# x + alpha * fx on one Trainium2 core: the first store held for 13 units of an addition, and a new order and placing of the loads

## The chip, the cores and the metric

The kernel runs on one core of a Trainium2 chip. The metric is the time of one execution in device microseconds (us). The core has 16 DMA engines that move data between its DRAM and its on-chip memory SBUF (128 partitions), and compute engines of which this kernel uses VectorE (DVE in the profile) for nearly all of its arithmetic. SyncE (SP) issues every transfer here. SP goes through its instructions in order: one that waits holds up all behind it.

## The reference

```python
B, S, D = 512, 32, 640            # x and fx: bf16; alpha: one bf16 number
def reference(x, fx, alpha):
    return x + alpha * fx
```

Each of x, fx and the output has 512 x 32 x 640 bf16 elements, 20.97 MB. Nothing is used twice, so 41.94 MB have to be read and 20.97 MB written.

## The kernel before

All three tensors are seen as 128 rows, one for each partition, and each row is cut into N = 160 units of K = 512 elements (1 KiB). One SBUF tile, `buf`, has room for ALL = 207 units in each partition, fewer than the 320 of both inputs, so places are used again. The tables F and X (lines 17 and 18) say where units of fx and of x stand: (first unit, end, home in buf). `at` (line 79) turns a range of units into a slice of `buf` by them. The last two pieces of each table are put over places whose fx units an earlier addition has read: those loads wait for that addition.

The order of the work is written out by hand, as lines of `PLAN` (line 23). Each line is one step, and the steps are emitted top to bottom:

- `f` and `x` issue a load of fx or x from SP (lines 88 and 92); in the kernel before, the number is the piece's place in the table. `s` issues a store (line 108) of a range in the table S.
- `a` loads alpha and brings it to all 128 partitions with one small matrix product (lines 110 to 118).
- `m a b` multiplies units a to b of fx by alpha in place, on VectorE (line 97).
- `t a b` adds fx's units a to b to x's in place, on VectorE (line 104). What the stores write are these sums, out of x's homes.

Each engine takes its steps in the order of PLAN. Waits follow from the data: a multiplication waits for its load, an addition for its load and the multiplication, a load for the last reader of the place that it overwrites, a store for the additions of its range. All transfers share one queue, so the DMA engines take them in the order of issue, each engine eight rows (partitions) of every transfer. A row is one contiguous piece of DRAM: a load of 64 units has 128 rows of 64 KiB, one of 32 units has rows of 32 KiB.

Up to the last load the DMA engines see this order: fx 0 to 8, fx 8 to 64, alpha, x 0 to 64, fx 64 to 96, x 64 to 96, fx 96 to 128, x 96 to 128, fx 128 to 160, x 128 to 160; then the stores of units 0 to 64, 64 to 128 and 128 to 160. The first store's data are complete early, when the additions `t 32 64` and `t 0 32` are through. On SP it stands right behind the last load.

Of the kernel before, what the change touches and what calls it, by code (L numbers as in the profile page):

```python
# [1 line left out]

# [4 lines left out]

ACT = mybir.ActivationFunctionType
ALU = mybir.AluOpType
F32 = mybir.dt.float32  # L10
BF16 = mybir.dt.bfloat16

K = 512
P = 128


F = [(0, 8, 96), (8, 64, 104), (64, 96, 160), (96, 128, 128), (128, 160, 175)]
X = [(0, 64, 0), (64, 96, 64), (96, 128, 96), (128, 160, 143)]
S = [(0, 64), (64, 128), (128, 160)]
N = 160  # L20
ALL = 207

PLAN = """
f 0
f 1
a
x 0
f 2
x 1
m 0 64  # L30
t 32 64
t 0 32
f 3
x 2
m 64 96
t 79 96
f 4
t 64 79
m 96 128
t 111 128  # L40
x 3
t 96 111
m 128 160
t 128 160
s 0
s 1
s 2
"""


@with_exitstack
def kernel(
    ctx: ExitStack,
    tc: tile.TileContext,
    x: bass.AP,
    fx: bass.AP,
    alpha: bass.AP,
    out: bass.AP,
):
    nc = tc.nc  # L60
    xv = x.flatten_outer_dims().rearrange("(p n) d -> p (n d)", p=P)
    fxv = fx.flatten_outer_dims().rearrange("(p n) d -> p (n d)", p=P)
    ov = out.flatten_outer_dims().rearrange("(p n) d -> p (n d)", p=P)
    assert xv.shape[1] == N * K

    consts = ctx.enter_context(tc.tile_pool(name="consts", bufs=1))
    psum = ctx.enter_context(tc.tile_pool(name="psum", bufs=1, space=bass.MemoryType.PSUM))
    whole = ctx.enter_context(tc.tile_pool(name="whole", bufs=1))
    ctx.enter_context(tc.manual_schedule())

    sync = mybir.DependencyInfo(mybir.DependencyClass.Sync, mybir.DependencyReason.DATA)
    buf = whole.tile([P, ALL * K], x.dtype, name="buf")
    done = []
    lanes = {}

    def units(v, a, b):
        return v[:, a * K : b * K]

    def at(pieces, a, b):

        s, _, h = next(p for p in pieces if p[0] <= a < p[1])
        e, _, g = next(p for p in pieces if p[0] < b <= p[1])
        assert h - s == g - e
        return units(buf, a + h - s, b + h - s)

    def load_f(i):
        a, b, _ = F[i]
        done.append(nc.sync.dma_start(out=at(F, a, b), in_=units(fxv, a, b)))  # L88

    def load_x(i):  # L90
        a, b, _ = X[i]
        done.append(nc.sync.dma_start(out=at(X, a, b), in_=units(xv, a, b)))

    def multiply(a, b):
        term = at(F, a, b)
        done.append(
            nc.vector.tensor_scalar(  # L97
                out=term, in0=term, scalar1=lanes["a_f"][:], scalar2=None, op0=ALU.mult
            )
        )  # L100

    def total(a, b):
        s = at(X, a, b)
        done.append(nc.vector.tensor_tensor(out=s, in0=s, in1=at(F, a, b), op=ALU.add))  # L104

    def store(i):
        a, b = S[i]
        done.append(nc.sync.dma_start(out=units(ov, a, b), in_=at(X, a, b)))

    def alpha_to_lanes():  # L110
        a_1 = consts.tile([1, 1], alpha.dtype, name="a_1")
        done.append(nc.sync.dma_start(out=a_1[:], in_=alpha[None, :]))  # L112
        ones = consts.tile([1, P], alpha.dtype, name="ones")
        nc.vector.memset(ones[:], 1.0)  # L114
        a_ps = psum.tile([P, 1], F32, name="a_ps")
        done.append(nc.tensor.matmul(a_ps[:], ones[:], a_1[:], start=True, stop=True))  # L116
        lanes["a_f"] = consts.tile([P, 1], F32, name="a_f")
        nc.vector.tensor_copy(out=lanes["a_f"][:], in_=a_ps[:])  # L118

    does = {  # L120
        "f": load_f,
        "x": load_x,
        "a": alpha_to_lanes,
        "m": multiply,
        "t": total,
        "s": store,
    }
    for step in PLAN.split("\n"):
        if step:
            what, *of = step.split()  # L130
            does[what](*map(int, of))

    rest = nc.sync.nop(nofuse=True)
    for i in done[:-1]:
        tc.add_manual_dep(rest.ins, i.ins.name, sync, reason="all but the last store")


# [1 line left out]
_INS = ['x', 'fx', 'alpha']  # L139
_OUTS = [((512, 32, 640), 'bfloat16')]  # L140


# [23 lines left out]
```

## Time and profile before

The median of three runs is 151.65 us (151.59 to 151.67). The profile below is of one execution.

| what | value |
|---|---|
| time of the profiled execution | 151.67 us |
| its span | 149.89 us |
| DMA engines busy | 98.0% of the span |
| bytes moved | 62.92 MB, 420 GB/s over the span |
| VectorE busy | 65.9 us (44%), 13 instructions |
| additions: 32, 17, 15 units | 8.69, 4.69, 4.15 us each |
| multiplications: 64, 32 units | 8.75, 4.48 us each |

How to read what follows: the page gives busy time of each engine, then the span in 40 slices with a digit for each (tenths of the slice), then the DMA queue, then the chain of waits that ended last. In the list in order of time, a line has the start, the duration, the engine, the line of the kernel, the operation and what it writes and reads; "SPq" lines are issues of transfers, whose rows move later. A table of windows gives, for each stretch between two times, the busy time of each engine and how many instructions began there, the granted clock, the mean busy share of the DMA engines and the rate in GB/s. Bytes are counted where a row starts, so windows that hold whole rows are the ones to compare.

### The profile page before, as it was taken

The page shows a single profiled execution, that of the slowest core. Times are in us where ns is not written, and L with a number is a line of the kernel's source. Part 1 is how long each engine was busy: PE and PEld are TensorE (multiplying, and loading weights), DVE is VectorE, ACT ScalarE, POOL GpSimd, SP SyncE. Part 2 cuts the span into 40 slices and gives each one's busy share as a digit, 9 for nine tenths or more (in the row PEclk, how much of TensorE's full clock was granted, in tenths as well). Part 3 has the DMA queues.
Part 4 walks back from the last instruction along what each step waited for, and adds up shares of the span by engine and source line. Part 5 has one row for each costly group of instructions (what it writes and reads, how often), then busy time and mean ns, then how long its engine had stood idle before and what let it go on. Part 6 is the DMA issues. An engine that isn't in the chain of part 4 may idle for free.

```text
span 149.9 us, 84 instructions
## 1 busy us (share of the span) xinstructions
PE 0.2 (0%) x1; PEld 0.1 (0%) x1; DVE 65.9 (44%) x13; POOL 0.2 (0%) x4
## 2 busy tenths in 40 slices
PE   0000000000000000000000000000000000000000
PEld 0000000000000000000000000000000000000000
DVE  0000009930079999999954998309920000000000
POOL 0000000000000000000000000000000000000000
DMA  5979996969899999999999999998998969697994
GB/s 164 606 337 398 490 525 280 560 280 560 376 437 437 428 420 420 420 420 420 428 463 463 437 437 428 420 420 367 472 490 350 560 280 560 280 560 315 455 446 184
DMA packets 1730, 62.92 MB, mean 420 GB/s; under 512 B 194, under 2 KB 194, under 8 KB 194
## 3 DMA queue, kind: packets, MB, share of 16 engines
q1 hardware_dynamic: 1730, 62.92, 98.0%
HBM read 41.94 MB, written 20.97 MB: 420 GB/s over the span
## 4 chain that ended last, share of the span: by engine, by line
DMA 51%; DVE 20%; SPq 1%; issue 0%; DVEq 0%
DMA buf<-in_x_dram 51%; DVE buf L104 20%; SPq L88 1%; SPq L112 0%; DVEq L104 0%
## 5 line engine op out<-in xcount | busy, mean ns | idle before, releaser
L104 DVE TENSOR_TENSOR buf<-buf 128x16384 bf16<-128x16384 bf16 (+2 forms) x7 | 43.5, 6251 | 20.5 <-DMA buf<-in_x_dram 20.5
L97 DVE TENSOR_SCALAR buf<-buf,a_f 128x16384 bf16<-128x16384 bf16 (+1 forms) x4 | 22.2, 5550 | 0.9 <-DMA buf<-in_fx_dram 0.9
L118 DVE COPY a_f<-a_ps 128x1 f32<-128x1 f32 x1 | 0.2, 157 | 21.5 <-PE a_ps L116 21.5
L114 DVE MEMSET ones<- 1x128 bf16 x1 | 0.2, 165 | 0.8 <-PEq L150 0.8
L116 PE MATMUL a_ps<-a,ones 1*128 1x1 bf16 x1 | 0.2, 158 | 22.3 <-DMA a<-in_alpha_dram 22.3
L150 POOL MEMSET const-bfloat16-1.0<- 128x1 bf16 x1 | 0.1, 101 | 0.0
L150 POOL MEMSET const-uint8-127<- 128x1 uint8 x1 | 0.1, 101 | 0.0
L150 POOL MEMSET const-float32-0.0<- 128x1 f32 x1 | 0.1, 98 | 0.2 <-issue 0.2
L150 POOL MEMSET const-float32-1.0<- 128x1 f32 x1 | 0.1, 98 | 0.0
L116 PEld LDWEIGHTS <-ones 1*128 1x128 bf16 x1 | 0.1, 97 | 1.0 <-DVE ones L114 1.0
## 6 DMA issues: line engine op xcount, KB each, us to landing
buf<-in_fx_dram SPq DMA_DIRECT2D x3, 4096.0 KB, 22.0
buf<-in_x_dram SPq DMA_DIRECT2D x3, 4096.0 KB, 21.4
buf<-in_fx_dram SPq DMA_DIRECT2D x1, 7168.0 KB, 21.4
out_dram<-buf SPq DMA_DIRECT2D x1, 4096.0 KB, 39.5
buf<-in_fx_dram SPq DMA_DIRECT2D x1, 1024.0 KB, 4.9
out_dram<-buf SPq DMA_DIRECT2D x2, 49.8
a<-in_alpha_dram SPq DMA_DIRECT2D x1, 0.0 KB
buf<-in_x_dram SPq DMA_DIRECT2D x1, 39.9
```

The source lines that it names most:

```text
L88: done.append(nc.sync.dma_start(out=at(F, a, b), in_=units(fxv, a, b)))
L97: nc.vector.tensor_scalar(out=term, in0=term, scalar1=lanes["a_f"][:], scalar2=None, op0=ALU.mult)
L104: done.append(nc.vector.tensor_tensor(out=s, in0=s, in1=at(F, a, b), op=ALU.add))
L114: nc.vector.memset(ones[:], 1.0)
L116: done.append(nc.tensor.matmul(a_ps[:], ones[:], a_1[:], start=True, stop=True))
L118: nc.vector.tensor_copy(out=lanes["a_f"][:], in_=a_ps[:])
L150: nc = _bacc.Bacc("TRN2", target_bir_lowering=False, num_devices=1)
```

## The change

There are four parts. Units 64 to 128 of fx come in one load instead of two. The places in `buf` are other ones: fx 0 to 64 at 128, fx 64 to 128 at 64, fx 128 to 160 at 111; x 64 to 128 at 143 and x 128 to 160 at 79. The order of the steps follows from that: the loads are now fx 0 to 8, fx 8 to 64, alpha, x 0 to 64, fx 64 to 128, x 96 to 128, x 64 to 96, fx 128 to 160, x 128 to 160, and an addition of 15 units (64 to 79), cut into 13 and 2, is left over until after the multiplication of the last units. And the first store gets a wait that its data do not ask for: `LATE` ties the issue of `s 0 64` to the end of `t 64 77`. Steps now name unit ranges instead of places in tables. The rest is another spelling: each step returns its instruction, which is kept under the step's text so that `LATE` can find it.

```diff
-F = [(0, 8, 96), (8, 64, 104), (64, 96, 160), (96, 128, 128), (128, 160, 175)]
-X = [(0, 64, 0), (64, 96, 64), (96, 128, 96), (128, 160, 143)]
-S = [(0, 64), (64, 128), (128, 160)]
+F = [(0, 64, 128), (64, 128, 64), (128, 160, 111)]
+X = [(0, 64, 0), (64, 128, 143), (128, 160, 79)]
 N = 160
 ALL = 207
 
 PLAN = """
-f 0
-f 1
+f 0 8
+f 8 64
 a
-x 0
-f 2
-x 1
+x 0 64
+f 64 128
 m 0 64
 t 32 64
+x 96 128
 t 0 32
-f 3
-x 2
-m 64 96
+x 64 96
+m 64 128
+t 111 128
+f 128 160
+t 96 111
 t 79 96
-f 4
-t 64 79
-m 96 128
-t 111 128
-x 3
-t 96 111
+x 128 160
 m 128 160
+t 64 77
+t 77 79
+s 0 64
 t 128 160
-s 0
-s 1
-s 2
+s 64 128
+s 128 160
 """
+LATE = {"s 0 64": "t 64 77"}
...
+    def transfer(name, out, in_):
+        r = nc.sync.dma_start(out=out, in_=in_)
+        if name in LATE:
+            tc.add_manual_dep(r.ins, said[LATE[name]].ins.name, sync, reason="issue late")
+        return r
...
+    def load_f(a, b):
+        return transfer(f"f {a} {b}", at(F, a, b), rows(fx, a, b))
...
+    def store(a, b):
+        return transfer(f"s {a} {b}", rows(out, a, b), at(X, a, b))
...
-            does[what](*map(int, of))
+            said[step] = does[what](*map(int, of))
+            done.append(said[step])
```

More of the change, by code (lines that the diff above doesn't have):

```diff
@@ L60, with rows @@
     nc = tc.nc
[L61 to L64, printed above, removed]
+    def rows(t, a, b):
+        v = t.flatten_outer_dims().rearrange("(p n) d -> p (n d)", p=P)
+        assert v.shape[1] == N * K
+        return v[:, a * K : b * K]
     consts = ctx.enter_context(tc.tile_pool(name="consts", bufs=1))
@@ L83, in at, with load_x @@
         assert h - s == g - e
[L84 to L92, printed above, removed]
+        return buf[:, (a + h - s) * K : (b + h - s) * K]
+    def transfer(name, out, in_):
[5 more added lines that the diff above has]
+        return transfer(f"f {a} {b}", at(F, a, b), rows(fx, a, b))
+    def load_x(a, b):
+        return transfer(f"x {a} {b}", at(X, a, b), rows(x, a, b))
+    def store(a, b):
+        return transfer(f"s {a} {b}", rows(out, a, b), at(X, a, b))
     def multiply(a, b):
         term = at(F, a, b)
[L96 to L99, printed above, removed]
+        return nc.vector.tensor_scalar(
+            out=term, in0=term, scalar1=lanes["a_f"][:], scalar2=None, op0=ALU.mult
         )
@@ L103, in total @@
         s = at(X, a, b)
[L104 to L108, printed above, removed]
+        return nc.vector.tensor_tensor(out=s, in0=s, in1=at(F, a, b), op=ALU.add)
     def alpha_to_lanes():
@@ L117, in alpha_to_lanes @@
         lanes["a_f"] = consts.tile([P, 1], F32, name="a_f")
-        nc.vector.tensor_copy(out=lanes["a_f"][:], in_=a_ps[:])
+        return nc.vector.tensor_copy(out=lanes["a_f"][:], in_=a_ps[:])
     does = {
```

3 lines of the change are left out of this document (1 added, 2 removed).

## The prediction

> **What bounds the kernel now.** I read the page's head and busy times first, then the slices and the DMA queue, then the chain of waits, then the order of time around the last load, and last the bytes moved in short windows around the point where loads give way to stores.
>
> ```profile
> span 149.9 us, 84 instructions
> ...
> PE 0.2 (0%) x1; PEld 0.1 (0%) x1; DVE 65.9 (44%) x13; POOL 0.2 (0%) x4
> ...
> DMA  5979996969899999999999999998998969697994
> ...
> q1 hardware_dynamic: 1730, 62.92, 98.0%
> ...
> DMA 51%; DVE 20%; SPq 1%; issue 0%; DVEq 0%
> ```
>
> VectorE (DVE) works 65.9 us of 149.9. The 16 DMA engines are busy 98.0% of the span and move 62.92 MB, which is both inputs and the output once each. So the chain's "DVE 20%" must not be read as a price: the chain ends at the last addition (109.6 us), and behind that there are 40 us of stores. The end is set by the sum of all transfers, which run one behind the other on one queue of SyncE (SP). Time can be won or lost only where a DMA engine runs below its rate or has nothing to do. The windows show where that is (columns: stretch, its us, busy time and count of each engine, clock, share of the DMA engines, GB/s):
>
> ```profile
> 1.74:4.74 3.00, 0.00 (x0) 0.00 (x0) 0.00 (x0) 0.00 (x0) 1.00 0.98 336
> ...
> 89.47:91.90 2.43, 0.00 (x0) 0.00 (x0) 1.55 (x2) 0.00 (x0) 1.00 1.01 432
> 91.90:94.33 2.43, 0.00 (x0) 0.00 (x0) 2.43 (x1) 0.00 (x0) 1.00 1.00 432
> 94.33:96.76 2.43, 0.00 (x0) 0.00 (x0) 0.67 (x1) 0.00 (x0) 1.00 1.00 432
> 96.76:99.92 3.16, 0.00 (x0) 0.00 (x0) 0.00 (x0) 0.00 (x0) 1.00 1.01 332
> ...
> 104.76:109.60 4.84, 0.00 (x0) 0.00 (x0) 4.84 (x1) 0.00 (x0) 1.00 1.00 433
> ```
>
> From 89.47 us the last load of x (units 128 to 160, eight rows of 32 KiB on each DMA engine) runs. Two rows take 2.43 us three times, at 432 GB/s; the last two take 3.16 us, at 332 GB/s. That is 0.73 us lost on each engine, right before the first store, while VectorE does nothing at all (0.00), so it is not VectorE's doing. The stores behind it run at 433 GB/s. The same rows' records give a mean of 0.76 us. The only other loss is the start of the queue: 1.74 to 4.74 us, at 336 GB/s, which against 433 is 3.00 x 97 / 433 = 0.67 us. What stands around that turn in order of time:
>
> ```profile
> 85.59 0.33 SPq L92 DMA_DIRECT2D buf<-in_x_dram  x1
> 86.02 23.96 SPq L108 DMA_DIRECT2D out_dram<-buf  x3
> 90.52 4.49 DVE L97 TENSOR_SCALAR buf<-buf,a_f 128x16384 bf16<-128x16384 bf16 x1 [0.88 <-DMA buf<-in_fx_dram]
> 100.92 8.69 DVE L104 TENSOR_TENSOR buf<-buf 128x16384 bf16<-128x16384 bf16 x1 [5.92 <-DMA buf<-in_x_dram]
> ```
>
> The last load is issued at 85.59 and the first store at 86.02, so the store stands in the queue all the time that the load's rows move. Reading it as cause: an engine that has finished reading the load's last rows goes on to read the store's source out of the same SBUF into which it still writes those rows.
>
> **The change part by part.**
>
> *One row of 64 KiB for fx units 64 to 128.* Before, they are two transfers of 32 KiB rows. By the records a 32 KiB row takes 1.2135 us and a 64 KiB row 2.418; per engine 16 x 1.2135 = 19.416 against 8 x 2.418 = 19.344, and one completion record of 0.009 less: 0.08 us won, on the path. x units 64 to 128 still come as two transfers, in the opposite order, so nothing is won there.
>
> *New order and homes: does the queue run dry among the loads?* Durations of VectorE come from its rows by form: a multiply of 64 units 8.75, of 32 units 4.48; additions of 32, 17 and 15 units 8.69, 4.69, 4.15. A line through the additions (0.5208 ns an element and 155 ns) gives 3.62 us for 13 units and 0.69 for 2. In order: the 64-unit fx transfer ends at 60.71 (60.79 before, less 0.08) and is told as landed some 0.56 later; the multiply runs 61.30 to 70.06; x 96 to 128 lands at 70.98, its 17-unit addition ends at 75.76, and so fx 128 to 160 is issued at 75.78, with the queue full until 80.1. x 64 to 96 lands at 80.70, its 17 units end at 85.48, and x 128 to 160 is issued at 85.50, with work until 89.8. Both lead by 4.3 us; before, the last load (85.59, work until 89.90) had as much, and no row there was stretched. The two x loads further up are issued at 50.73 and 59.34, right after additions that the diff leaves in place, with work until 60.7 and 70.4. So this costs nothing; the cover is those 4.3 us. VectorE waits 2 us more for the whole fx transfer, which its idle time takes in. SP issues one transfer fewer (11 instead of 12, beside alpha's), of some 0.3 us at the start, beside the first loads.
>
> *The hold.* fx 128 to 160 lands at 90.41; the multiply runs 90.44 to 94.92, the 13 units 94.94 to 98.56, and the first store is issued at 98.58 instead of 86.02. Behind it on SP wait only the two other stores: the second needs the 2 units more (99.25), the third the last addition (109 us); each has the 19.3 us of a store before it as cover. The last addition is moved past nothing that it needs: x 128 to 160 lands at about 100 either way.
>
> What the hold does to the turn is the disputed price. The slowest engine sets the end. In the records of before it starts its first store row at 100.48; without the stretch it would have ended its load at 99.74, with the 0.08 at 99.66. The only row of an empty queue taking up work is the start: first load issued at 0.73, first row at 1.74, so 1.01 us; the 16 engines begin over another 0.39 us, and by the window above the start loses 0.67 us in all, this spread included, until the rows run at rate. The slowest engine ends its eighth row at 5.28; less 8 x 0.309 that is a start at 2.81, or 2.08 us after the issue.
>
> - From below: rows begin 1.01 us after the issue, at 99.59, before the slowest engine has run out (99.66), and nothing is stretched. It starts at 99.66 instead of 100.48: 0.82 us won.
> - From above: the store begins as badly as the first load: 98.58 + 2.08 = 100.66, 0.18 us lost.
> - I take 1.01 + 0.39, a start at 99.98, so 0.50 us won: the issue and the spread over the engines belong to any transfer, while the slow rows after it (2.08 less 1.40, 0.68 us) I put down to reads from DRAM into idle engines; the store reads SBUF, and most engines are still at work. That last is a choice; no row shows a store that starts late.
>
> The Trainium skill ("DMA: Bandwidth & Descriptors", section "Latency and other measured facts") gives about 0.6 us to the first byte for a transfer of this kind. The trace has 1.01 us at its only dry start, and the trace decides; by the skill's figure the rows would be there at 99.18 and the sum would be the lower end, 150.85 us.
>
> **Sum.** The profiled execution took 151.67 us (span 149.89 and 1.78 around it), 0.02 above the median of 151.65. 151.67 - 0.50 (0.08 of it from the longer rows) = 151.17, and I say 151.2. No change that can be told is 0.2%, 0.3 us: 151.35 to 151.95.
>
> **The rivals.**
>
> 1. *Wash.* Either the stretch belongs to the turn itself (each engine changes from writing SBUF to reading it, however late the store is told), and then the load ends at 100.4 as before and only 0.08 is won: 151.6; or the late start costs what the stretch did: by the upper bound 151.67 + 0.18 = 151.85. For it: the loss of 0.73 and the start's loss of 0.67 us are alike in size. Against the first half: where one load follows another, no row of the records is stretched, though the engines pass there from one transfer to the next just so.
>
> 2. *Slower: the store must be read before it can be written.* Queued early, the store's first rows were read while the load's were written; issued at 98.58, they can't be. If an engine has to take in its whole first row of 64 KiB, 2.42 us by its own record, before it writes, the slowest starts at 99.98 + 2.42 = 102.40 instead of 100.48: 1.92 lost, 153.6 us. It decides from 0.8 us of such reading on (100.78). For it: the stretch begins two whole rows ahead of the turn, which looks like reading far ahead. Against it: the first load's 8 KiB rows begin to end within 0.9 us of their start, and 64 KiB rows follow 56 KiB rows without a gap. The Trainium skill's "Rules for kernel authors" on the same page says to issue a DMA early, so that its fixed setup cost overlaps; the hold is the opposite, and by that rule the time comes out on this side. The trace bears it out at the start alone, with 1.01 us from the first issue to the first row; there is no late store in it.
>
> 3. *The hold does nothing*, since the store would wait for something else anyway: excluded by 86.02, where it was issued with all of its data done.
>
> **How the numbers follow.** The hold pays by 0.3 us or more (slowest engine starts by 100.2): 0.52. Wash: 0.28. Slower by over 0.3 us: 0.20. So faster 0.52, same 0.28, slower 0.20. The range runs from 150.85, the lower bound, to 152.0, which takes in the upper bound (151.85) and the near edge of the second rival; its far part is left out. The likeliest case alone lies between 150.85 and 151.35.
>
> **What would show it.** Right: the windows over the last two rows of the last load come back to about 432 GB/s; the first store is issued near 98.6; no load's window is below 430; the stores end about 0.5 us earlier. Wrong: the 332 GB/s are still there (the turn's own), or the rows are at rate but a window of low GB/s lies behind the last load (the dry start), or an issue of a load comes later than the queue runs out.

## The result, and the profile after

The changed kernel takes 150.97 us (median of 6 runs, 150.91 to 151.15) against 151.59 us for the kernel before, run beside it (6 runs, 151.46 to 151.67). The ratio is 0.9962, with a 95% interval of 0.9949 to 0.9975: 0.38% faster, 0.6 us. Forecast were 151.2 us, a range of 150.85 to 152.0, and 0.52 for "faster". The profiled execution took 151.14 us.

The page after, its head, VectorE's busy time and the DMA queue:

```profile
span 149.4 us, 83 instructions
...
PE 0.2 (0%) x1; PEld 0.1 (0%) x1; DVE 65.9 (44%) x13; POOL 0.2 (0%) x4
...
q1 hardware_dynamic: 1586, 62.92, 97.9%
```

VectorE does the same 65.9 us of work and the same 62.92 MB move, in 1586 records of the DMA engines instead of 1730, since the longer fx rows are fewer. The share of the DMA engines is 97.9%, 0.1 points lower than before. That share alone would not show the gain: a stretched row counts as busy. The order of time around the last load:

```profile
85.48 0.33 SPq L86 DMA_DIRECT2D buf<-in_x_dram  x1
90.55 4.49 DVE L102 TENSOR_SCALAR buf<-buf,a_f 128x16384 bf16<-128x16384 bf16 x1 [5.10 <-DMA buf<-in_fx_dram]
94.95 4.22 DVE L108 TENSOR_TENSOR buf<-buf 128x6656 bf16<-128x6656 bf16 x2
98.60 10.72 SPq L86 DMA_DIRECT2D out_dram<-buf  x3
```

The store is issued at 98.60 instead of 86.02, behind the 13 units (128x6656). The windows that answer to those of before, cut at the rows of the last load (the four busy times are those of PE, PEld, DVE and POOL, in this order):

```profile
94.24:96.67 2.43, 0.00 (x0) 0.00 (x0) 2.43 (x2) 0.00 (x0) 1.00 1.00 432
96.67:99.10 2.43, 0.00 (x0) 0.00 (x0) 2.43 (x2) 0.00 (x0) 1.00 1.00 432
99.11:99.44 0.33, 0.00 (x0) 0.00 (x0) 0.06 (x1) 0.00 (x0) 1.00 0.02 0
99.44:101.87 2.43, 0.00 (x0) 0.00 (x0) 1.60 (x1) 0.00 (x0) 1.00 1.02 432
104.28:109.12 4.84, 0.00 (x0) 0.00 (x0) 4.68 (x1) 0.00 (x0) 1.00 1.00 433
```

The last two rows of the last load take 2.43 us at 432 GB/s; they took 3.16 at 332. In exchange there is a stretch that was not there before: from 99.11 us, when the first engine has ended its load, until 99.44 no new data row begins. It is short, and engines that end later lose less by it: the last one ends its load at 99.72 and begins its store row at 99.75.

### The profile page after: what moved, and what is told of

Same layout as the page of the kernel before. It is cut to its first block, busy times and chain, and to the rows that moved or that the text cites. A ratio compares the mean times of both kernels' runs of the same rounds, so it can differ in the third digit from the quotient of the medians.

```text
span 149.4 us, 83 instructions
## 1 busy us (share of the span) xinstructions
PE 0.2 (0%) x1; PEld 0.1 (0%) x1; DVE 65.9 (44%) x13; POOL 0.2 (0%) x4
## 2 busy tenths in 40 slices
DMA packets 1586, 62.92 MB, mean 421 GB/s; under 512 B 178, under 2 KB 178, under 8 KB 178
## 3 DMA queue, kind: packets, MB, share of 16 engines
q1 hardware_dynamic: 1586, 62.92, 97.9%
## 4 chain that ended last, share of the span: by engine, by line
DMA 51%; DVE 21%; SPq 1%; issue 0%; DVEq 0%
DMA buf<-in_x_dram 51%; DVE buf L108 21%; SPq L86 1%; SPq L112 0%; DVEq L108 0%
## 5 line engine op out<-in xcount | busy, mean ns | idle before, releaser
L108 DVE TENSOR_TENSOR buf<-buf 128x16384 bf16<-128x16384 bf16 (+4 forms) x8 | 43.7, 5488 | 13.6 <-DMA buf<-in_x_dram 13.6
L102 DVE TENSOR_SCALAR buf<-buf,a_f 128x32768 bf16<-128x32768 bf16 (+1 forms) x3 | 22.0, 7331 | 7.2 <-DMA buf<-in_fx_dram 7.1
```

The source lines that it names most:

```text
L102: return nc.vector.tensor_scalar(out=term, in0=term, scalar1=lanes["a_f"][:], scalar2=None, op0=ALU.mult)
L108: return nc.vector.tensor_tensor(out=s, in0=s, in1=at(F, a, b), op=ALU.add)
```

## The experiments

The theory: a store that is issued (told to the queue) early stands right behind the last load in the queue and stretches that load's last rows by about 0.7 us; the hold takes the stretch away, as long as the store's rows still come before the engines run out. The rivals: the new order, homes and longer row carry the gain; or a late start costs nothing; and, as the runs went on, several readings of what makes the stretch.

### The hold undone, and the hold alone

```diff
-LATE = {"s 0 64": "t 64 77"}
+LATE = {}
```

> The changed kernel with the hold alone undone: the first store waits for its data only. Theory (a store that stands in the queue stretches the last load's rows): it is issued near 85.9 us, the last two rows of the last load take about 3.16 us instead of 2.43 (332 GB/s), and only the 0.08 us of the longer fx rows is left: ratio to before 0.9995. Rival (order, homes and the longer row carry the gain): ratio 0.996 as with the hold.

Measured: 151.60 us, ratio 1.0004 (0.9995 to 1.0013). The store is issued at 85.71. The window over the last two rows, until the first engine is through, in this kernel:

```profile
96.78:99.54 2.76, 0.00 (x0) 0.00 (x0) 2.25 (x2) 0.00 (x0) 1.00 1.06 380
```

The stretch is back, if not at the 3.16 us that were expected: 2.76 us for the first engine through, and 0.48 us as the mean of all engines by the rows' records. That mean is less than the 0.76 of before, but the last engine, which sets the end, ends its load at 100.34, against 100.47 before, and the time is the same. The other direction, the hold put into the kernel before, with its own loads and homes; the left-over units are 96 to 111 here, since no later load waits for them:

```diff
-t 96 111
 m 128 160
+t 96 109
+t 109 111
+s 0
 t 128 160
-s 0
...
-        done.append(nc.sync.dma_start(out=units(ov, a, b), in_=at(X, a, b)))
+        r = nc.sync.dma_start(out=units(ov, a, b), in_=at(X, a, b))
+        if i == 0:
+            tc.add_manual_dep(r.ins, done[-2].ins.name, sync, reason="issue late")
+        done.append(r)
```

(`done[-2]` is the step before the last one, `t 96 109`.)

> The kernel before with the hold alone: its own loads, homes and order, only the additions of units 96 to 111 moved behind the last multiplication and cut into 13 and 2, and the first store held for the 13. Theory: issue near 98.7 us, the last two rows at 432 GB/s, 0.5 to 0.6 us won, ratio 0.9963 to 0.9968. Rival (order, homes, longer row): ratio 1.000.

Measured: 151.07 us, ratio 0.9967 (0.9954 to 0.9979). The last two rows:

```profile
96.87:99.29 2.42, 0.00 (x0) 0.00 (x0) 2.24 (x2) 0.00 (x0) 1.00 1.01 433
```

So the hold alone gives the gain, and all the rest together, without it, gives nothing that can be told. The 0.08 us that the longer fx rows were to give is within the interval of both runs, so the times can't show it. The records show less: from the mean start of the place in the queue that fx 64 to 128 takes to the mean start of the transfer behind it are 19.37 us before and 19.35 after (19.34 without the hold), a gain of 0.02 to 0.03 us.

### How long to hold

Four kernels cut the left-over 15 units at another place and hold the store for the first part, of 5, 7, 9 or 11 units (the edit below is that of 9). One holds it for all 15 (`LATE` names `t 77 79`), and one releases it after the last multiplication (`LATE` names `m 128 160`):

```diff
-t 64 77
-t 77 79
+t 64 73
+t 73 79
-LATE = {"s 0 64": "t 64 77"}
+LATE = {"s 0 64": "t 64 73"}
```

> The changed kernel with the first store held only until the last multiplication, so issued near 94.95 us, 4.7 us before the slowest engine runs out. Theory: the store is in the queue before the last two rows begin (96.7 us), they are stretched in full, ratio 0.9995. Rival (any hold helps, since SP or VectorE gets the time): ratio 0.996.

> The changed kernel with the first store held for all 15 left-over units, 0.69 us longer, so issued near 99.28 us. Theory: its rows come 0.84 us after the issue, at 100.12, when the slowest engine has run out at 99.70; they begin 0.4 to 0.7 us later than with 13 units and that is lost: ratio 0.999 to 1.001. Rival (a late start costs nothing by itself, the engines catch up): ratio 0.996.

> The changed kernel with 9 instead of 13 units of the left-over addition ahead of the first store, so issued near 97.5 us; its rows could begin at 98.35, up to 1.35 us before the slowest engine runs out. Theory (rows are stretched as long as a told store and unwritten load rows are together): part of the stretch, about half of it, 0.3 to 0.4 us: ratio 0.998 to 0.999. Rival (the stretch is all or nothing, from the first store that is told before the last rows begin at 96.7): ratio 0.996.

> The changed kernel with 11 units ahead of the first store, issued near 98.05 us. First theory, corrected after 9 units (the store's reads hurt only while the load's own reads from DRAM are still coming in, and these are over a microsecond or more before the last writes): no stretch, and the store's rows are there at 98.9, before any engine has run out: ratio 0.993 to 0.994, as with 9 units, and better than with 13. Rival (9 units won for another reason, and 13 has already nothing to lose but idle 0.3 us on the first engines): ratio 0.996.

> 7 units ahead of the first store, issued near 96.75 us, its reads from some 97.5 us, 1.5 to 2 us before the last writes of the load. Corrected theory: a part of the stretch, up to 0.3 us, ratio 0.994 to 0.996. Rival (all or nothing by whether the store is told before the last two rows begin, 96.5 to 97.1): nothing or nearly nothing, ratio 0.9935, or the whole 0.7 us, ratio 1.000.

> 5 units ahead of the first store, issued near 96.2 us, its reads from some 97.0 us, 2 to 2.5 us before the last writes of the load. Corrected theory: most of the stretch is back, 0.4 to 0.6 us, ratio 0.997 to 0.999. Rival (all or nothing): 0.9935 or 1.000.

| held for | store issued at, us | median, us | ratio to before (95%) |
|---|---|---|---|
| its data only | 85.71 | 151.60 | 1.0004 (0.9995 to 1.0013) |
| the last multiplication | 95.03 | 151.65 | 1.0004 (0.9995 to 1.0013) |
| 5 units | 96.26 | 151.30 | 0.9970 (0.9956 to 0.9984) |
| 7 units | 96.74 | 150.79 | 0.9937 (0.9918 to 0.9956) |
| 9 units | 97.28 | 150.74 | 0.9934 (0.9921 to 0.9946) |
| 11 units | 97.76 | 150.80 | 0.9932 (0.9917 to 0.9948) |
| 13 units (the change) | 98.60 | 150.97 | 0.9962 (0.9949 to 0.9975) |
| 15 units | 99.20 | 151.59 | 0.9998 (0.9990 to 1.0007) |

Each ratio is to runs of the kernel before made beside it. The kernels held for their data, the multiplication or 15 units ran on one chip, 9 units on a second, and 5, 7 and 11 units on a third.

Both edges stand in the windows. Released after the multiplication, the stretch is whole; with 5 units little of it is left; with 7 none (one window of each, over the last two rows of the last load):

```profile
96.82:99.86 3.04, 0.00 (x0) 0.00 (x0) 2.32 (x2) 0.00 (x0) 1.00 1.02 345
```

```profile
96.50:99.00 2.50, 0.00 (x0) 0.00 (x0) 2.47 (x1) 0.00 (x0) 1.00 1.01 419
```

```profile
96.53:98.95 2.42, 0.00 (x0) 0.00 (x0) 2.38 (x2) 0.00 (x0) 1.00 1.01 433
```

With 5 units the records show the last row of ten engines untouched and of six longer (1.24 to 1.69 us instead of 1.215). The slowest engine sets the end, so its 0.4 us count, while the window shows the first. Single runs spread with 5 units from 150.94 to 151.86, more than with any other: the release stands on the edge. With 7 units five of six runs took 150.73 to 150.82 us and one 151.41, so the edge may not be far.

With 9 and 11 units the records show no loss on either side. Of 9 units, the last two rows of the load and the two 64 KiB rows behind:

```profile
96.54:98.96 2.42, 0.00 (x0) 0.00 (x0) 2.38 (x2) 0.00 (x0) 1.00 1.01 433
98.96:103.80 4.84, 0.00 (x0) 0.00 (x0) 3.78 (x1) 0.00 (x0) 1.00 1.00 433
```

With 15 units the queue does run dry. The rows at rate, then the time in which the engines run out one after the other, then 0.33 us in which none has anything to do, then the store:

```profile
96.85:99.28 2.43, 0.00 (x0) 0.00 (x0) 2.32 (x2) 0.00 (x0) 1.00 1.00 432
99.30:99.70 0.40, 0.00 (x0) 0.00 (x0) 0.00 (x0) 0.00 (x0) 1.00 0.02 0
99.71:100.04 0.33, 0.00 (x0) 0.00 (x0) 0.00 (x0) 0.00 (x0) 1.00 0.00 0
100.04:104.88 4.84, 0.00 (x0) 0.00 (x0) 4.63 (x1) 0.00 (x0) 1.00 1.01 433
```

What follows. The gain is a plateau of a microsecond, from 96.7 to 97.8 us of issue, and is gone at 95.0 on the one side and at 99.2 on the other. The theory as first put ("rows are stretched as long as a told store and unwritten load rows are together") fell with 9 units: there the store is told 1.7 us before the first engine has written its load, and no row is longer. The theory as corrected after that (only reads of the store that come while the load is itself still being read do harm) asked for up to 0.3 us of stretch with 7 units, and none came; with 5 units it asked for 0.4 to 0.6 us, and the slowest engine lost 0.4. Its rival there, all or nothing, fell with those 5 units, where six engines lose a part. The rival "any hold helps" fell with the multiplication, "a late start costs nothing" with 15 units. The 13 units of the change lie on the late edge. That 9 and 11 beat 13 is clear from the records within one execution: from the slowest engine's last load row to the end of the last store it takes 48.53 us with 13 units (99.72 to 148.25), 48.33 with 9 (99.46 to 147.79) and 48.33 with 11 (99.40 to 147.73), so 0.2 us. The ratios say 0.4 us, but 13 and 9 were not measured beside each other, and their intervals nearly meet (0.9949 and 0.9946). In the two profiles, too, the loads of 9 units end 0.26 us earlier (99.46 against 99.72), ahead of anything that the hold could change.

Where these 0.2 us go can be read from the records. In the three kernels whose store is told at 98.5 us or later (13 units in either kernel, and 15 units) the first 64 KiB row of the store takes 2.46 to 2.48 us as the mean of the engines, the fifteen behind it take 2.424 us each, and the last eight, of 32 KiB, 1.217. Told earlier, they take 2.418 and 1.213. The fifteen rows together take 36.32 us with 13 or 15 units, and 36.22 with 9, with 11 and in the kernel before (means of the engines). So a start that comes too late costs more than the idle time itself; why the later rows are slower stays open.

### What makes the stretch

Three kernels without the hold ask what it hangs on. In the first, the first store takes its data from DRAM instead of SBUF:

```diff
-LATE = {"s 0 64": "t 64 77"}
+LATE = {}
...
-return transfer(f"s {a} {b}", rows(out, a, b), at(X, a, b))
+return transfer(f"s {a} {b}", rows(out, a, b), rows(x, a, b) if a == 0 else at(X, a, b))
```

> The changed kernel without the hold, where the first store takes units 0 to 64 of x from DRAM instead of the sums out of SBUF, so those units of the output are x; the window over the last two rows of the last load is what counts, not the time. Theory (the store's reading of SBUF beside the load's writing into SBUF makes the stretch): no stretch, about 432 GB/s. Rival (any store that stands behind a load, by its writing to DRAM or its place in the queue): 332 GB/s.

The store is issued at 85.56, as early as without the hold, and the load's last two rows are not stretched:

```profile
96.55:98.97 2.42, 0.00 (x0) 0.00 (x0) 2.32 (x2) 0.00 (x0) 1.00 1.00 433
99.43:109.00 9.57, 0.00 (x0) 0.00 (x0) 8.69 (x1) 0.00 (x0) 1.00 0.98 336
```

(The second line is the copy from DRAM to DRAM itself, at 336 GB/s, which is why this kernel takes 156.39 us.) So neither the place in the queue nor the writing into the output is enough to make the stretch; it needs the source in SBUF. This rests on one execution, in which no engine's last row of the load takes more than 1.216 us.

In the second, the first store is cut into 8 and 56 units:

```diff
-s 0 64
+s 0 8
+s 8 64
...
-LATE = {"s 0 64": "t 64 77"}
+LATE = {}
```

> The changed kernel without the hold, the first store cut into units 0 to 8 (rows of 8 KiB) and 8 to 64 (56 KiB). Theory with a read ahead counted in bytes: the 56 KiB rows follow at once, the stretch stays at about 0.7 us, ratio 1.000. Theory with a read ahead counted in rows (one or two rows): only 8 to 16 KiB are read early, 0.2 us or less of stretch, ratio 0.997.

Measured: 151.78 us, ratio 1.0001 (0.9992 to 1.0010), and the stretch is the largest seen behind the last load, 0.86 us in the window:

```profile
96.52:99.81 3.29, 0.00 (x0) 0.00 (x0) 2.46 (x2) 0.00 (x0) 1.00 1.01 319
```

Short rows at the head of the store don't help, and a read ahead of one or two rows is excluded. Whether what is read early goes by bytes, by time or by a larger number of rows the run can't tell: the eight rows of 8 KiB on each engine are together as long as one of 64 KiB.

In the third the first store is put ahead of the last load of x, so that loads give way to stores twice:

```diff
+s 0 64
 x 128 160
...
-s 0 64
...
-LATE = {"s 0 64": "t 64 77"}
+LATE = {}
```

> The changed kernel without the hold and with the first store put between the last load of fx and the last load of x, so that loads give way to stores twice. Theory (each turn from loads to a store queued behind them stretches the last rows by 0.7 us): ratio near 1.005 if going from stores back to loads is free. Rival (the stretch belongs to the last load of all, where no load follows to keep reading): ratio 1.000.

Measured: 152.08 us, ratio 1.0020 (1.0011 to 1.0029). The windows over the two rows before the first turn, those at the first turn, and those at the second (store 64 to 128 issued at 99.94, the load's rows until 120.0):

```profile
84.43:86.86 2.43, 0.00 (x0) 0.00 (x0) 0.70 (x1) 0.00 (x0) 1.00 1.00 432
86.86:90.32 3.46, 0.00 (x0) 0.00 (x0) 0.00 (x0) 0.00 (x0) 1.00 1.02 303
116.90:119.32 2.42, 0.00 (x0) 0.00 (x0) 0.00 (x0) 0.00 (x0) 1.00 1.02 433
```

The first turn costs the first engine 1.03 us, more than before; the second, which has the same kind of load and a store told long ahead, next to nothing (eleven engines keep 1.213 us in the last row, five take 1.225 to 1.44). Neither the theory nor its rival had that. By the slowest engine the first turn costs 1.23 us (its load ends at 90.90 instead of 89.67) and the second 0.1, together 0.6 more than the 0.73 of the kernel before. The time rose by 0.2%, 0.3 us; in this profile the loads ahead of the first turn also run 0.3 us earlier than in that of the kernel before, so the sum fits only with that start. Going from stores back to loads shows no cost: the load's first rows take 1.213 us.

One guess was that any store that has run before frees the later turn. So one unit of the first store, rows of 1 KiB, was put there instead of the whole:

```diff
+s 0 1
 x 128 160
...
-s 0 64
+s 1 64
...
-LATE = {"s 0 64": "t 64 77"}
+LATE = {}
```

> The changed kernel without the hold, with 1 unit of the first store (rows of 1 KiB) taken out and put between the last load of fx and the last load of x. What is asked is why the second turn of the kernel with two turns had no stretch. Theory (what counts is that no other store had come before: once stores have run between loads, the DRAM reads are no longer far ahead): a small stretch of 0.3 us or less at the small store, none at the large one, ratio 0.996 to 0.998. Rival (a turn is a turn, and the second was free for another reason): about 0.7 us at the large store as well, ratio 1.000 to 1.004.

Measured: 151.64 us, ratio 0.9992 (0.9982 to 1.0003). The rows ahead of the small store, and those ahead of the large one:

```profile
86.96:89.39 2.43, 0.00 (x0) 0.00 (x0) 0.00 (x0) 0.00 (x0) 1.00 1.00 432
96.99:100.24 3.25, 0.00 (x0) 0.00 (x0) 1.96 (x2) 0.00 (x0) 1.00 1.00 323
```

The small store, 8 KiB on each engine, stretches nothing; the large one behind the last load stretches as ever (0.82 us). The guess fell as put. Why the second turn of the kernel with two turns is all but free stays open; a long run of stores between the loads is what these two kernels don't share.

## Why the prediction was right, point by point

- *What bounds the kernel.* Right: the sum of the transfers on one queue, and the only loss in the middle of it was the 0.73 us ahead of the first store. Undoing the hold brings the whole time back, and holding too long gives it back, as idle engines and as slower rows behind them.
- *The longer fx rows, 0.08 us.* Too much: the records show 0.02 to 0.03 us at that place in the queue (19.37 to 19.35 or 19.34). The 64 KiB rows there take 2.421 us as their mean, not the 2.418 of the sum. No time confirms or denies so little. The 60.79 that the prediction gives as the end of the transfer is not that of the slowest engine, which ends at 60.88.
- *The queue among the loads.* Right: the last load is issued at 85.48 (85.50 worked out), and no row among the loads behind the start of the queue is longer by more than 0.02 us.
- *The hold's issue.* 98.60 against 98.58 worked out.
- *The disputed price.* The first store row was put 1.01 us after the issue and the last engine's start another 0.39 later, at 99.98. Measured: 0.84 us (99.44), and the last engine at 99.75. So the choice not to charge the queue's start in full was right: the slow rows of the start are of the start. With 15 units, where all engines are idle, the dry start of a store can be read alone: rows begin 0.84 to 1.00 us after the issue, and the first takes 2.48 instead of 2.42 us. The upper bound (2.08 us from issue to work) was twice too dear. The slowest engine's 0.73 us (100.48 to 99.75) would have given more than the 0.50 forecast; 0.2 of it is lost again in the stores behind the late start, to which the prediction gave no term, and the time fell by 0.62 in the medians and 0.53 between the two profiled executions. Two misses of 0.2 us, of opposite sign, made the sum come out: the way of the gain was right, its nearness to the number is in part luck. One sign of being wrong that the prediction named did show, in small: the window without new rows behind the last load (99.11 to 99.44), since 13 units stand on the late edge.
- *The rival "wash".* Its first half, a stretch that belongs to the turn itself, fell with 7 to 11 units, where the turn costs nothing. Its second half, a late start as dear as the stretch, is not what 13 units show, but what 15 do (0.9998).
- *The rival "the store must be read before it can be written".* Fell: dry or not, the first 64 KiB row begins with no such wait and is 0.06 us longer, not 2.42. The Trainium skill's rule to issue a DMA early ("DMA: Bandwidth & Descriptors", "Rules for kernel authors") does not hold for this store: told at 85.7 or 95.0 us the ratio is 1.0004, told at 97.3 us it is 0.9934. What is right in it is the other edge: told 0.5 us before the first engine runs out (13 units) the start-up of 0.84 us shows, told 1.2 us before (11 units) it does not.
- *The rival "the hold does nothing".* Excluded as worked out: the issue moved from 86.02 to 98.60 us.
- *The first-byte figure.* The Trainium skill ("DMA: Bandwidth & Descriptors", "Latency and other measured facts") has about 0.6 us to the first byte. The dry store shows 0.84 us from the start of its issue to its first row, between that and the 1.01 of the first load.
- *The reading of the cause* was too wide. It said that an engine reads the store's source out of the SBUF into which it still writes the load. With 9 units the store is told 1.7 us, and by the 0.84 us could be moving 0.85 us, before the first engine is through, and the rows keep 1.215 us each. The source in SBUF is needed (with DRAM as the source there is no stretch), but whatever it disturbs is over some time before the load's last writes.

## What to carry to other kernels

On a queue that never runs dry, look at the rate in windows cut at whole rows, not at the busy share: the loss sat in rows that took 1.7 instead of 1.2 us while the engines counted as busy. Where loads give way to stores that are ready long before, try to hold the first store until one to two microseconds before the first engine has written the load, by tying it to an instruction whose end is known, and sweep that point: here the free stretch was one microsecond wide, with the whole gain gone 1.4 us behind it and 1.7 us ahead of it. The best points here were 7 to 11 units (ratio 0.993 to 0.994), not the 13 of the change; choose the middle of the plateau, since with 5 units, on its edge, single runs spread over 0.9 us.

## What the runs showed of the hardware that was not expected

In these runs a DMA engine that has the last load from DRAM and behind it a store out of SBUF in its queue writes the last 64 KiB of that load at a lower rate, 0.5 to 1.1 us later as the mean of the engines (303 to 380 GB/s in the windows instead of 432). It does so only if the store was told early enough: at 95.03 us in full, at 96.26 on six of sixteen engines, at 96.74 on none, where the engines end the load between 98.95 and 99.45. If the store's reads begin 0.84 us after the issue, the time to the first row that was measured on idle engines, then reads that begin about 2 us before the load's last write disturb it, and those that begin 1.4 to 1.9 us before it don't. That fits an engine whose own reads of the load are over some 2 us ahead of its last write and are held up by reads of SBUF that come among them; the runs show the times and the need of an SBUF source, and this reading of them is argued only. Not explained is the second turn of the kernel with two turns, behind a long store, where the slowest engine loses 0.1 us and most lose nothing.

The second thing is the price of a late start. Where the engines had run out or nearly so when the store's rows came (issue at 98.54 to 99.20 us), all later 64 KiB rows took 2.424 us instead of 2.418, some 0.2 us over the stores with the slower first row. The three profiles show it and no other does; why is open.
